# Channel attention and a multiplicative FFN on one core: an order chosen from an account of free times, and seven products instead of eight for half the blocks of the last batch

## The chip, the cores and the metric

The kernel runs on one core of one Trainium2 chip. The metric is the device time of the whole program in microseconds (us), the median of several executions. A second figure, the span, comes from one profiled execution and runs from its first to its last instruction. Engines are named as in the profile: PE (TensorE, matmuls), PEld (its weight loads), DVE (VectorE), ACT (ScalarE), POOL (GpSimd) and SP (SyncE, which here only issues DMAs).

## The reference

```python
def _attn_ref(q, k, v, tau):                      # (4, 5824, 256) each, tau = 1
    qn = q / (np.linalg.norm(q, axis=1, keepdims=True) + 1e-06)
    kn = k / (np.linalg.norm(k, axis=1, keepdims=True) + 1e-06)
    s = kn.transpose(0, 2, 1) @ qn / tau          # 256 x 256 per batch
    s = s - s.max(-1, keepdims=True)
    a = np.exp(s)
    a /= a.sum(-1, keepdims=True) + 1e-09
    return (v @ a).astype(np.float32)

def _moe_ref(x, w1, w2, w3, w_out):               # x: 23296 x 256, d_ff = 1024
    a = x @ w1
    b = x @ w2
    h = a * b @ w3
    return (h @ w_out).astype(np.float32)
```

The result is 23296 x 256 in fp32. The FFN takes the output of the attention as `x`, with its four batches laid one after the other.

## The kernel before

Two foldings make the work small. `w3 @ w_out` is made once (`W_sb`, 1024 x 256, by `w_unit`), and for each batch the 256 x 256 attention matrix is folded into `w1` and `w2` (`fold_mm`; the result is `Wf`). What is left per token is `a = v @ Wf[0]`, `b = v @ Wf[1]`, the product `a * b`, and its product with `W_sb`.

A batch is cut into 12 chunks of tokens (`NCH`): eleven of 512 tokens and a last one of 192. `v` is loaded in pieces of two chunks, turned by a transposing DMA on SP's queue (`transpose_piece`), and used as the moving operand. A block is one chunk `c` and one tile `j` of 128 of the 1024 columns of d_ff, so a full chunk has 8 blocks. `emit_ab` makes a block: two matmuls of 512 columns for `a` and two for `b` (two halves of the 256 input channels, L657), each pair into a PSUM bank of its own; ACT copies `a` to SBUF in bf16 (`as`, L663) and DVE multiplies it with `b` (`abh`, L676). Four PSUM banks, `ab0` to `ab3`, are taken in fixed rotation.

When the 8 blocks of a chunk are done, its product with `W_sb` follows. `emit_half` does it plainly: 32 matmuls of 256 columns. `seven_products` does it by Winograd's form of Strassen's scheme: the 512 x 1024 block and the 1024 x 256 matrix are cut in 2 x 2, four sums of blocks of `abh` are made (`operand`, L589 and L592, tiles `S`; in batches 0 to 2 on POOL, in the last one on DVE), and seven products of 8 matmuls of 128 columns each take the place of eight (L570). ACT copies partial results out (L580), DVE adds others to them (L583), and SP stores the chunk. Before, chunks 0 to 3 of batch 0 and chunk 10 of batch 3 are done plainly, the chunks 11 have a form of their own (`emit_out`), and all others use seven products.

While batch b runs, the scores of batch b+1 are summed between its blocks (`score_units`: matmuls `G` L200, squares on ACT L197, sums `acc` on DVE L212), and near the end of batch b come its softmax and the folds. The last batch has no such work beside it.

The order of the whole program is written out by Python and kept as written; each engine runs its instructions in that order and waits where an operand or a buffer isn't ready. Each block is a slot. What comes between blocks is chosen by counting slots (`pend` for output products with a lag of a few slots, `due_sums` for the sums `S`, `by_slot` for scores) and by a clock that adds up matmul costs (`agenda`, `run_due`: loads, transposes, softmax, folds). No count is kept of when ACT, DVE or POOL will be done.

Of the kernel before, what the change touches and what calls it, by code (L numbers as in the profile page):

```python
# [16 lines left out]
LAG = 2  # L17
LAG_END = 5
LAG_FAST = 4
BIG_BUFS = 21  # L20
# [5 lines left out]
def kernel(  # L26
# [82 lines left out]
    pieces = {}  # L109

# [8 lines left out]
    def load_part(nm, n, pi, lo, hi):  # L119
        nc.gpsimd.dma_start(  # L120
            out=pieces[nm, n, pi][:, lo:hi, :], in_=qk_main[nm, n][0][:, pi * PIECE + lo : pi * PIECE + hi, :]
        )
# [10 lines left out]
    def new_vT(n):  # L133
        vTs[n] = (
            vT_pool.tile([P, NT - 1, CT, P], BF16, tag="vT", name=f"vT_{n}"),
            vT_pool.tile([P, CT, P + LEFT], BF16, tag="vTt", name=f"vTt_{n}"),
        )
# [11 lines left out]
    def transpose_half_on_pe(n, pi, h, on_act):  # L149
        if pi == 0 and h == 0:  # L150
            new_vT(n)
        t = pieces["v", n, pi]
        i0 = 4 * h
        pe_transpose(
            vTs[n][0][:, pi * PIECE + i0 : pi * PIECE + i0 + 4, :, :].rearrange("p i c t -> p (i c) t"),
            [t[:, i0 + i, ct * P : (ct + 1) * P] for i in range(4) for ct in range(CT)],
            "out", on_act,
        )

    def transpose_piece(n, pi):  # L160
        if pi == 0:
            new_vT(n)
        vT, vTt = vTs[n]
        t = pieces.pop(("v", n, pi))
        if pi < NP_ - 1:
            nc.sync.dma_start_transpose(vT[:, pi * PIECE : (pi + 1) * PIECE, :, :], t[:, :, :])
        else:
            g = LAST - 1
            nc.sync.dma_start_transpose(vT[:, pi * PIECE : pi * PIECE + g, :, :], t[:, :g, :])

            first = n % 2 == 0
            nc.sync.dma_start_transpose(vTt[:, :, :P] if first else vTt[:, :, LEFT:], t[:, g, :])
            nc.sync.dma_start_transpose(vTt[:, :, P:] if first else vTt[:, :, :LEFT], t[:LEFT, g + 1, :])
# [6 lines left out]
    def score_units(n):  # L180
# [4 lines left out]
        def pair_unit(pr, part):  # L185
# [7 lines left out]
            if part < 2:  # L193
                if part == 0:
                    sqs[0] = work.tile([P, 2, 2, C], F32, tag="sq", name=f"sq_{n}_{pr}", bufs=2)
                src = qt if part == 0 else kt
                nc.scalar.activation(out=sqs[0][:, :, part, :], in_=src[:, o : o + 2, :], func=AF.Square)  # L197
# [10 lines left out]
            elif pr == 0:  # L208
                if part == 2:
                    nc.vector.tensor_add(accs[n], sqs[0][:, 0], sqs[0][:, 1])  # L210
            else:
                nc.vector.tensor_add(accs[n], accs[n], sqs[0][:, part - 2])  # L212

        sqs = [None]
# [62 lines left out]
    def soft_units(n):  # L277
# [142 lines left out]
        def fold_mm(key, c2, tag="ab", on_act=True):  # L420

            w, c1, lo, hi = key
            if c2 == 0:
                turn = (lo // 512 * 4 + w * CT + c1) % 3
                home = bank(tag) if n == 0 or turn == 2 else {"tag": ("out2", "G")[turn], "bufs": 1}
# [6 lines left out]
            if c2 == CT - 1:  # L432
                dst = Wf[n][:, c1, w, lo:hi]
                if on_act:
# [3 lines left out]

        def fold(i, tag="ab"):
            h, rest = divmod(i, 4)  # L440
            w, c1 = divmod(rest, 2)
# [35 lines left out]
        if n == 0:  # L477
            return [k_first, k_row, q_first, scaled_first, first_folds, second_quarter, sum_start, k_early] + [lambda i=i: fold(i, "ab" if i == 7 else "out") for i in range(4, 8)]
# [12 lines left out]
    clock = [0.0]  # L491
    agenda = []

    def run_due(upto=None):
        lim = clock[0] if upto is None else upto
        while agenda and agenda[0][0] <= lim:
            _, _, cost, fn = agenda.pop(0)
            clock[0] += cost
            fn()

# [9 lines left out]
    pend = []  # L510
# [4 lines left out]
    def rhs_of(b, c, ct):  # L515
        vT, vTt = vTs[b]
        if c < NCH - 1:
            return vT[:, 4 * c : 4 * c + 4, ct, :]
        return vTt[:, ct, :]

    last_ab = [None]
    halves = {}
    slot = [0]
    due_sums = []
    following = []
    comb = {}

    def seven(b, c):
        if b == B - 1:
            return c < NCH - 2  # L530
        return (4 if b == 0 else 0) <= c < NCH - 1

    def combine_weights(step):
# [15 lines left out]
        else:  # L549
            nc.vector.tensor_sub(T[:, 3], b21, f[:, 1])  # L550

    def seven_products(b, c, k1, k2):

        T = comb["T"]
# [5 lines left out]
        t1, t2, t3, t4 = ([T[:, i, j, :] for j in range(4)] for i in range(4))  # L560
        st, sums = {}, {}
        tags = {"A": "out0", "B": "out1", "C": "out1" if b < B - 1 else "out2"}
        adder = nc.gpsimd if b < B - 1 else nc.vector

        def product(nm, a, w, first=False):
# [8 lines left out]
            clock[0] += 8 * (P * MM_COL + MM_FIX)  # L574
# [4 lines left out]
        def keep(r, d):  # L579
            nc.scalar.copy(quarter(r, d), st["A"])  # L580

        def join(nm, r, d):
            nc.vector.tensor_add(quarter(r, d), st[nm], quarter(r, d))  # L583

        def operand(i):

            x = sums[i] = work.tile([P, 4, 2 * P], BF16, tag=f"S{i}", name=f"S{i}_{b}_{c}", bufs=1)
            if i == 1:
                adder.tensor_add(x, a21, a22)  # L589
            else:  # L590
                u, w = {2: (sums.get(1), a11), 3: (a11, a21), 4: (a12, sums.get(2))}[i]
                adder.tensor_sub(x, u, w)  # L592

        def p1():
            st["o"] = work.tile([P, 4, D], F32, tag="o_sb", name=f"osb_{b}_{c}", bufs=3)
            product("A", a11, w1, True)
            keep(0, 0)

        def p5():
            product("C", sums[1], t1, True)  # L600

        def p6():
            product("A", sums[2], t2)
            keep(0, 1)

        def p7():
            product("A", sums[3], t3)
            keep(1, 1)

        def p2():  # L610
            product("B", a12, w21, True)

        def p4():
            product("A", a22, t4)
            keep(1, 0)

        def p3():
            product("C", sums[4], w22)

        def store():  # L620
# [3 lines left out]
        def S(i):  # L624
            return lambda: operand(i)

        def J(*x):
            return lambda: join(*x)

        def then(fn):  # L630
            return lambda: following.append(fn)

        if b == B - 1:
            return [S(1)], [
                [S(2), p1], [S(3), p5], [p6], [S(4), p7], [J("C", 1, 1), p2],
                [J("B", 0, 0), p4], [p3, J("C", 0, 1), store],
            ]
        return [S(1), S(2), S(3), S(4)], [
            [p1], [p2, then(J("B", 0, 0))], [p6], [p5], [p7], [then(J("C", 1, 1))], [p4], [p3, then(J("C", 0, 1)), then(store)],
        ]  # L640

    def gate():

        if last_ab[0] is not None:
            nc.gpsimd.tensor_copy(gate_t, last_ab[0][:1, :1])  # L645

# [4 lines left out]
    def emit_ab(b, c, j):  # L651
        n = chunk_cols(c)
        tiles = []
        for w in range(2):
            t = psum.tile([P, 512], F32, name=f"{'ab'[w]}_{b}_{c}_{j}", **bank("ab"))
# [5 lines left out]
            tiles.append(t)  # L661
        a_sb = work.tile([P, 512], BF16, tag="a_sb", name=f"as_{b}_{c}_{j}", bufs=4)
        nc.scalar.copy(a_sb[:, :n], tiles[0][:, :n])  # L663
        if c == NCH - 1:
            if b % 2 == 0 and j == 0:
                lefts[b // 2] = work.tile([P, FT, 2, P + LEFT], BF16, tag="left", name=f"left_{b}", bufs=1)
            both = lefts[b // 2][:, j, b % 2, :]
            nc.vector.tensor_mul(both, a_sb[:, :n], tiles[1][:, :n])
            ab = both[:, :P] if b % 2 == 0 else both[:, LEFT:]
        else:  # L670
            if j == 0:
                halves[c] = [
                    in_pool.tile([P, 4, 512], BF16, tag="big", name=f"abh_{b}_{c}_{h}", bufs=BIG_BUFS) for h in range(2)
                ]
            ab = halves[c][j // 4][:, j % 4, :]
            nc.vector.tensor_mul(ab, a_sb, tiles[1])  # L676
        last_ab[0] = ab
        slot[0] += 1
        if not seven(b, c):
            if b == B - 1 or c == NCH - 1:  # L680
                lag = LAG if b == B - 1 else FT + LAG_FAST
                pend.append((slot[0] + lag, 1, lambda only=None: emit_out(b, c, j, ab, only)))
            elif j == FT - 1:
                for i in range(FT):
                    fn = lambda i=i, ab2=tuple(halves[c]): emit_half(b, c, i, ab2)
                    pend.append((slot[0] + 1 + LAG_FAST + i, 1, fn))
        elif j == FT - 1:
            sums, groups = seven_products(b, c, *halves[c])
            for i, fn in enumerate(sums):
                due_sums.append((slot[0] + 2 * i, fn))  # L690
            ready = slot[0] + 1 + (LAG_FAST if b < B - 1 else 0)
            for i, group in enumerate(groups):
                wait = 0 if b == B - 1 else i
                pend.append((ready + wait, 2, lambda group=group: [fn() for fn in group]))
        clock[0] += 4 * (n * MM_COL + MM_FIX)

    def emit_half(b, c, i, ab2):
# [13 lines left out]
        clock[0] += 4 * (D * MM_COL + MM_FIX)  # L711
        if i == 3:
            nc.scalar.copy(o[:, 0:2, :], t)
        elif i == FT - 1:
            nc.vector.tensor_copy(o[:, 2:4, :], t)
# [3 lines left out]
    def emit_out(b, c, j, ab, only=None):  # L719
# [23 lines left out]
        clock[0] += len(lhs) * (D * MM_COL + MM_FIX)  # L743
        if j == FT - 1:
            o = work.tile([P, 4, D], F32, tag="o_sb", name=f"osb_{b}_{c}", bufs=3)
# [283 lines left out]
```

## Time and profile before

| | us |
|---|---|
| median of 3 runs (555.11 to 555.23) | 555.18 |
| span of the profiled execution | 553.5 |
| PE busy | 542.1 |
| DVE busy | 435.5 |
| ACT busy | 375.8 |
| POOL busy | 304.8 |
| L657, matmuls of `a` and `b` with 512 columns (x1408) | 418.8 |
| L570, matmuls of the seven products, 128 columns (x2184) | 166.6 |

The median is 1.7 us above the span: this much lies around the instructions. Busy time of PE is not work done: matmuls overlap in the pipeline, a matmul of 512 columns is recorded with 379 ns and one of 128 columns with 219 ns, while the next one starts earlier than that. What a matmul costs on PE is the distance from its start to the start of the next, and that is read from a timeline.

Four batches follow each other: the blocks of batch 0 begin near 37 us, those of batch 1 near 165, of batch 2 near 300 and of batch 3 near 428, and the last matmul starts at 549.2 us. What comes before 37 us is the first batch's loads, scores and softmax.

### The profile page before, as it was taken

To read this page: it belongs to the slowest core of one execution; us is meant where nothing else is said; L and a number is where in the kernel's file an instruction comes from. 1 tells how busy PE (TensorE), PEld (TensorE's weight loads), DVE (VectorE), ACT (ScalarE), POOL (GpSimd) and SP (SyncE) were. 2 spreads that over 40 slices of the span, in tenths; PEclk is the share of its full clock that TensorE was granted. 3 is DMA by queue.
4 is the path that set the end of the run, shared out by engine and by line. 5 is a ranking of instruction groups with operands and counts; after the bars stand their busy time and mean duration, and the time that the engine had idled before them with its cause. 6 is when DMAs were issued, how large, how long until landed. Compare 5 with 4: busy or idle time off the path is not lost.

```text
span 553.5 us, 12330 instructions
## 1 busy us (share of the span) xinstructions
PE 542.1 (98%) x4630; PEld 352.9 (64%) x4630; DVE 435.5 (79%) x789; ACT 375.8 (68%) x757; POOL 304.8 (55%) x257
## 2 busy tenths in 40 slices
PE   7799999999999999999999999999999999999997
PEld 4564577766666666666667566666666666666665
DVE  5567747899976787988876788888877688988984
ACT  5436647788866777777766777777766666566663
POOL 4150022678889678889887588898987400010000
PEclk9999999999999999999999999999999999999999
DMA  9999888975666879576554777875650245343102
GB/s 213 211 206 209 167 164 201 224 180 82 152 140 155 191 150 165 126 147 136 128 127 122 153 153 156 164 147 124 147 115 40 83 117 117 91 110 82 77 40 97
DMA packets 74972, 77.61 MB, mean 140 GB/s; under 512 B 54176, under 2 KB 58784, under 8 KB 74912
## 3 DMA queue, kind: packets, MB, share of 16 engines
q0 software_dynamic: 15616, 38.93, 40.3%
q1 hardware_dynamic: 58928, 37.17, 24.2%
q8 instruction: 36, 0.59, 0.4%
q10 hardware_dynamic: 368, 0.72, 0.3%
q14 instruction: 24, 0.20, 0.1%
HBM read 78.91 MB, written 23.86 MB: 186 GB/s over the span
## 4 chain that ended last, share of the span: by engine, by line
PE 93%; DMA 5%; DVE 0%; ACT 0%; POOL 0%; issue 0%; POOLq 0%
PE a L657 28%; PE b L657 28%; PE prodA L570 13%; PE prodC L570 6%; PE G L200 5%; PE prodB L570 3%; DMA k<-in_k_dram 3%; PE o L707 3%; PE fold L428 2%; DMA q<-in_q_dram 2%; PE o_out L738 2%; PE w L882 1%; PE G L271 0%; PE narrow L452 0%; PE sqq L259 0%
## 5 line engine op out<-in xcount | busy, mean ns | idle before, releaser
L676 DVE TENSOR_TENSOR abh<-as,b 128x512 bf16<-128x512 bf16 x352 | 240.0, 684 | 82.0 <-ACT as L663 76.2
L663 ACT CAST as<-a 128x512 bf16<-128x512 f32 (+1 forms) x384 | 215.4, 562 | 94.8 <-PE a L657 61.5
L657 PE MATMUL a<-vT,Wf 128*128 128x512 bf16 x704 | 209.4, 379 | 0.1
L657 PE MATMUL b<-vT,Wf 128*128 128x512 bf16 x704 | 209.4, 379 | 0.0
L657 PEld LDWEIGHTS <-Wf 128*128 128x128 bf16 x1536 | 141.1, 98 | 100.6 <-issue 0.8
L570 PEld LDWEIGHTS <-S 128*128 128x128 bf16 x1248 | 82.6, 98 | 34.3
L212 DVE TENSOR_TENSOR acc<-acc,sq 128x512 f32<-128x512 f32 x132 | 91.6, 694 | 3.0 <-ACT sq L197 1.9
L580 ACT COPY osb<-prodA 128x256 f32<-128x256 f32 x156 | 58.1, 372 | 42.0 <-PE prodA L570 41.4
L589 POOL TENSOR_TENSOR S<-abh,abh 128x1024 bf16<-128x1024 bf16 x29 | 61.7, 2127 | 32.1 <-DVE abh L676 16.6
L570 PEld LDWEIGHTS <-abh 128*128 128x128 bf16 x936 | 62.0, 98 | 25.7 <-issue 0.2
L592 POOL TENSOR_TENSOR S<-S,abh 128x1024 bf16<-128x1024 bf16 x29 | 61.8, 2131 | 1.9
L592 POOL TENSOR_TENSOR S<-abh 128x1024 bf16<-128x1024 bf16 x29 | 61.8, 2131 | 0.1
L592 POOL TENSOR_TENSOR S<-abh,S 128x1024 bf16<-128x1024 bf16 x29 | 61.7, 2129 | 0.1
L645 POOL COPY gate_t<-abh 1x1 bf16<-1x1 bf16 x39 | 7.2, 185 | 80.1 <-DVE abh L676 79.9
L570 PE MATMUL prodA<-comb_T,S 128*128 128x128 bf16 x624 | 47.6, 219 | 0.0
L200 PE MATMUL G<-k,q 128*128 128x256 bf16 x276 | 47.0, 273 | 0.0
L197 ACT ACTIVATE sq<-q 128x512 f32<-128x512 bf16 x69 | 43.8, 634 | 0.0
L197 ACT ACTIVATE sq<-k 128x512 f32<-128x512 bf16 x69 | 43.4, 628 | 0.0
L583 DVE TENSOR_TENSOR osb<-prodC,osb 128x256 f32<-128x256 f32 x78 | 32.5, 417 | 0.0
L200 PEld LDWEIGHTS <-q 128*128 128x128 bf16 x276 | 23.9, 98 | 3.6
L570 PE MATMUL prodB<-W_sb,abh 128*128 128x128 bf16 x312 | 23.8, 219 | 0.1
L570 PE MATMUL prodC<-comb_T,S 128*128 128x128 bf16 x312 | 23.8, 219 | 0.0
(139 smaller groups left out, 444.0 us busy)
## 6 DMA issues: line engine op xcount, KB each, us to landing
out_dram<-osb SPq DMA_DIRECT2D x44, 512.0 KB, 3.2
k<-in_k_dram POOLq DMA_DIRECT2D x19, 512.0 KB, 8.3
v<-in_v_dram POOLq DMA_DIRECT2D x19, 512.0 KB, 5.2
q<-in_q_dram POOLq DMA_DIRECT2D x18, 512.0 KB, 5.8
w_wout<-in_moe_w_dram POOLq DMA_DIRECT2D x1, 2048.0 KB, 21.6
k<-in_k_dram POOLq DMA_DIRECT2D x4, 320.0 KB, 6.5
v<-in_v_dram POOLq DMA_DIRECT2D x4, 320.0 KB, 5.4
q<-in_q_dram POOLq DMA_DIRECT2D x3, 320.0 KB, 5.2
```

The lines of the kernel that those rows point to most:

```text
L197: nc.scalar.activation(out=sqs[0][:, :, part, :], in_=src[:, o : o + 2, :], func=AF.Square)
L200: nc.tensor.matmul(G[:, ct, :], lhsT=qt[:, i, ct * P : (ct + 1) * P], rhs=kt[:, i, :], start=(pr == 0 and part == 0 and ct == 0), stop=(pr ...
L212: nc.vector.tensor_add(accs[n], accs[n], sqs[0][:, part - 2])
L570: nc.tensor.matmul(st[nm][:, i, :], lhsT=a[:, j, i * P : (i + 1) * P], rhs=w[j], start=(first and j == 0 and i == 0), stop=(j == 3), skip_ ...
L580: nc.scalar.copy(quarter(r, d), st["A"])
L583: nc.vector.tensor_add(quarter(r, d), st[nm], quarter(r, d))
L589: adder.tensor_add(x, a21, a22)
L592: adder.tensor_sub(x, u, w)
L657: nc.tensor.matmul(t[:, :n], lhsT=Wf[b][:, ct, w, j * P : (j + 1) * P], rhs=rhs_of(b, c, ct), start=(ct == 0), stop=(ct == CT - 1),)
L663: nc.scalar.copy(a_sb[:, :n], tiles[0][:, :n])
L676: nc.vector.tensor_mul(ab, a_sb, tiles[1])
L707: nc.tensor.matmul(t[:, k, :], lhsT=ab2[j // 4][:, j % 4, (2 * h + k) * P : (2 * h + k + 1) * P], rhs=W_sb[:, j, :], start=(j == 0 and k = ...
```

## The change

The change does three things.

First, the order. Slots, lags and the clock are replaced by an account of free times: `now` holds a time for PE, ACT, DVE and POOL, `free` one for each PSUM bank, and `work_on` adds the cost of each instruction as it is written. The program is split into lines that stop after each group of matmuls and say when the next group can start: `normal` (a block, in two halves), `by_seven` (below), `seven_products` or `plain_products` (a chunk's output). `step` takes the line that can start first. Banks are taken by `open_bank`, the one that is free first, instead of in rotation; in the last batch `out2` and `G` join the four. Sums on POOL wait in a list (`pool_line`) and are written when POOL is free by the account.

Second, in the last batch chunks 0 to 9 are taken two at a time, and for 4 of the 8 tiles `j` of such a pair `a` and `b` of both chunks come from `by_seven`: seven products of 512 columns instead of eight. It needs four sums of blocks of the turned `v` per pair (`token_sum`, on POOL) and four sums of blocks of `Wf`, once (`weight_sums`, on DVE from the PSUM banks of the folds).

Third, smaller things that come with it. The sums `S` are made on POOL in the last batch too. Five chunks of the last batch are done plainly (0, 2, 6, 9, 10) instead of one. `seven_products` starts its bank B with a copy of A by ACT, which saves one addition on DVE. The turned `v`, the sums `S`, and `w3` with `w_out` move into the common pool of buffers `big` (31 instead of 21), so `w3` and `w_out` are loaded by five DMAs instead of two. Some loads and scores get earlier places.

```diff
+HALF_BACK = 12
-BIG_BUFS = 21
+BIG_BUFS = 31
...
+    BY_SEVEN = {(3, c): 4 for c in range(0, 10, 2)}
+    PLAIN = {0: (0, 1, 2, 3), 1: (), 2: (), 3: (0, 2, 6, 9, 10)}
+    now = {"PE": 0.0, "ACT": 0.0, "DVE": 0.0, "POOL": 0.0}
+    LATE = {"PE": 0.205, "ACT": 0.155, "DVE": 0.135, "POOL": 0.1}
...
+    def work_on(engine, cost, *after):
+        now[engine] = max(now[engine], *after, 0.0) + cost
+        return now[engine] + LATE[engine]
...
+    def token_sum(b, c, i):
...
+        b11, b12, b21, b22 = (rhs_of(b, c + d, ct) for ct in range(CT) for d in range(2))
+        if i == 0:
+            nc.gpsimd.tensor_sub(t[:, 0], b12, b11)
+        elif i == 1:
+            nc.gpsimd.tensor_sub(t[:, 1], t[:, 0], b22)
+        elif i == 2:
+            nc.gpsimd.tensor_sub(t[:, 2], b22, b12)
+        else:
+            nc.gpsimd.tensor_add(t[:, 3], b21, t[:, 1])
...
+    def by_seven(b, c, j):
...
+        xt, X = take(f"X_{b}_{c}_{j}", True)
+        r = mm512(X, W[:, 0, 0, js], rhs_of(b, c, 0), True)
+        yt, Y = take(f"Y_{b}_{c}_{j}", True, True)
+        nc.scalar.copy(Y, X)
...
+        tt, t = take(f"T_{b}_{c}_{j}")
+        r = mm512(t, S[0][:, js], T[:, 0], True)
+        t5 = work.tile([P, 512], F32, tag="t5", name=f"t5_{b}_{c}_{j}", bufs=2)
+        nc.scalar.copy(t5, t)
...
+        r = mm512(X, S[1][:, js], T[:, 1], False)
+        zt, Z = take(f"Z_{b}_{c}_{j}", True, True)
+        nc.vector.tensor_add(Z, X, t5)
...
+        r = mm512(Y, W[:, 1, 0, js], rhs_of(b, c, 1), False)
+        a0 = cast(Y, f"as_{b}_{c}_{j}")
...
+        r = mm512(X, S[2][:, js], T[:, 2], False)
+        b1 = work.tile([P, 512], BF16, tag="b_sb", name=f"bs_{b}_{c + 1}_{j}", bufs=2)
+        nc.vector.tensor_add(b1, X, t5)
...
+        r = mm512(Z, S[3][:, js], rhs_of(b, c + 1, 1), False)
+        h1 = place(b, c + 1, j)
+        nc.vector.tensor_mul(h1, b1, Z)
...
+        r = mm512(X, W[:, 1, 1, js], T[:, 3], False)
+        h0 = place(b, c, j)
+        nc.vector.tensor_mul(h0, a0, X)
...
+    def step(b, todo, sevens, at_n):
...
+        choices = [(max(now["PE"], w.est()), i, w) for i, w in enumerate(lines["W"])]
+        if lines["N"] is not None:
+            choices.append((max(now["PE"], lines["N"].est()) + 0.08, 3, lines["N"]))
+        if outs:
+            hurry = credit[0] > 0.0 or steps_left[0] > 2 * HALF_BACK or not todo
+            choices.append((max(now["PE"], outs[0].est()) + (-0.02 if hurry else 0.2), 4, outs[0]))
...
+        when, kind, line = min(choices, key=lambda x: x[:2])
...
-    SLOTS0, SLOTS = (37, 78), (4, 71)
+    SLOTS0, SLOTS = (37, 76), (3, 66)
...
-            moves = [("qk", n, 1, 1), ("v", b, 2, 7), ("qk", n, 2, 19), ("v", b, 3, 25), ("qk", n, 3, 37)]
+            moves = [("qk", n, 1, 1), ("v", b, 2, 5), ("qk", n, 2, 16), ("v", b, 3, 23), ("qk", n, 3, 31)]
```

## Prediction, made before the changed kernel ran

> **What bounds the kernel now.** I read the page's busy table and its chain of waits first, then PE's waits, then busy time by batch, then one stretch of the timeline.
>
> ```profile
> PE 542.1 (98%) x4630; PEld 352.9 (64%) x4630; DVE 435.5 (79%) x789; ACT 375.8 (68%) x757; POOL 304.8 (55%) x257
> PE 93%; DMA 5%; DVE 0%; ACT 0%; POOL 0%; issue 0%; POOLq 0%
> ```
>
> PE is named in 93% of the chain that ended last, DMA (the first loads) in 5%, DVE, ACT and POOL in none. What PE waited for:
>
> ```profile
> PE sqq L259 <- DMA q<-in_q_dram: 4.7, 4, 1.7
> PE warm_I-94_95 L230 <- DVE ones_pp L87: 1.4, 1, 1.4
> PE sqq L259 <- ACT q L804: 0.4, 1, 0.4
> PE sum L405 <- ACT e L385: 0.4, 1, 0.4
> PE sqk L259 <- DMA k<-in_k_dram: 0.2, 1, 0.2
> ```
>
> All of it lies in the first 37 us, where the change does nothing. By batch (columns: stretch, its length, busy us and count of PE, PEld, DVE, ACT, POOL, granted clock, DMA share, GB/s):
>
> ```profile
> 37.00:165.00 128.00, 128.00 (x974) 82.01 (x974) 103.21 (x174) 91.11 (x176) 60.48 (x60) 1.00 0.85 171
> 165.00:300.00 135.00, 134.92 (x1200) 88.11 (x1198) 108.43 (x201) 100.69 (x209) 112.91 (x81) 1.00 0.69 145
> 300.00:428.00 128.00, 128.00 (x1125) 83.42 (x1123) 103.18 (x188) 95.17 (x196) 104.15 (x75) 1.00 0.62 134
> 428.00:549.00 121.00, 120.98 (x1081) 78.50 (x1079) 99.76 (x178) 72.85 (x148) 9.67 (x12) 1.00 0.32 89
> ```
>
> PE is full in every batch, and in the last one POOL is nearly idle. But pipelined matmuls look busy even when they start late, so I took start-to-start distances: 0.216 us for 512 columns, 0.109 for 256, 0.056 for 128 (medians). Against 2.4 columns per ns plus 2.5 ns for each matmul, all starts from 60 to 549 us together lose 1.6 us, mostly at the joins of the batches. So the middle holds almost no waiting that an order could recover; time falls only with columns.
>
> The latencies for a chain come from a stretch near the end:
>
> ```profile
> 538.24 0.59 PE L657 MATMUL b<-vT,Wf 128*128 128x512 bf16 x2
> 538.44 0.58 ACT L663 CAST as<-a 128x512 bf16<-128x512 f32 x1 [0.72 <-DVE abh L676]
> 538.67 0.61 PE L570 MATMUL prodA<-comb_T,abh 128*128 128x128 bf16 x8
> 539.06 0.69 DVE L676 TENSOR_TENSOR abh<-as,b 128x512 bf16<-128x512 bf16 x1 [0.29 <-ACT as L663]
> 539.12 0.59 PE L657 MATMUL a<-vT,Wf 128*128 128x512 bf16 x2
> ```
>
> The pair for `a` gives way to `b` at 538.24, and ACT begins 0.20 later; ACT takes 0.58, DVE starts 0.04 after it and takes 0.69.
>
> **What the Trainium skill says.** "TensorE: Matmul & The Clock Gate", section "Wait — 56ns, not 53.3ns?", gives start-to-start as N / 2.4 GHz plus about 2.5 ns when warm. The trace agrees (0.216, 0.056). The page "SBUF — State Buffer", section "Who interferes with whom", says that a DVE operation with two SBUF inputs contends with a GpSimd one that reads SBUF, and one with a single SBUF input does not. The change brings GpSimd work into the last batch; the DVE operations of its blocks read one operand from PSUM and one from SBUF. L676, of that kind, shows no effect: 684 ns on average (240.0 us for 352), 59.90 us for its 88 with POOL 84% busy (165 to 300 us) and 60.19 with POOL 8% busy (428 to 549 us). So I add nothing for POOL's presence. "VectorE: DVE Perf Modes", section "The TRN2 errata — SBUF-src ops pay a fixed extra latency per instruction", gives (N+151)/0.96 ns for an fp32 addition, 691 ns at 512; the row of `acc` (L212, one PSUM and one fp32 SBUF operand) shows 694.
>
> **PE's work.** By the order of instructions of the two kernels:
>
> - a and b. 20 pairs of blocks (5 pairs of chunks, 4 tiles each) lose one of 8 matmuls of 512 columns: 20 x 0.2158 = 4.32 us less.
> - Output. Four more chunks are done plainly: 32 matmuls of 256 columns (32 x 0.1092 = 3.49) instead of 56 of 128 (56 x 0.0558 = 3.13): 4 x 0.367 = 1.47 us more.
> - All else is the same on PE: scores, folds, `w_unit`.
>
> Net 2.85 us less. The totals agree: 1245259 columns and 4616 matmuls become 1239115 and 4500, so 6144 / 2400 + 116 x 0.0025 = 2.56 + 0.29 = 2.85.
>
> **The other engines in the last batch**, whose PE stretch shrinks to about 118 us:
>
> - DVE: 99.8, less 40 products of L676 (27.4), 40 sums S (27.4) and 30 additions L583 (12.5); plus 80 operations of the new blocks at 0.69 (55.2) and 12 additions L583 (5.0): 92.7 us, 79%. Back to back such operations start 0.60 apart, so there is more room than this says.
> - ACT: 72.9, plus 20 more copies of 512 net (11.7), less 40 output copies at 0.372 (14.9), plus 30 such for the six chunks of sevens (11.2), plus 8 plain copies at 0.586 (4.7): 85.6 us, 73%. The copy `Y` goes from PSUM to PSUM, which the trace doesn't show; 0.56 (the form mean of L663) to 0.63 (an ACT operation that reads SBUF, L197); I take 0.58.
> - POOL: 24 sums at 2.13 and 20 token sums of half that size at half that time (no row; 0.7 to 1.4, I take 1.07): 72.5 us, 61%.
>
> None becomes the bound on average. The 8 weight sums on DVE (no row; 0.69 to 0.75 by L212 and L437) fall at the end of batch 2, where 4 scalings go to ACT: 3 us more on a DVE with 20% free.
>
> **What the new order adds in waits.** I took each place in PE's order as the sum of what stands before it at the prices above, and compared each hand-over with the latencies read. Three are short:
>
> - A block of sevens copies `X` to `Y` and PE then goes on with `X`: end of the first matmul, 0.20, 0.58, about 0.05, so 0.83. For the pair of chunks 2 and 3 (tile 1) only 0.54 us of other matmuls lie between: 0.29 lost; four others lack 0.08. About 0.3 in sum.
> - At the end, the plain output of chunk 10 comes right behind chunk 9's last group and waits for its copy: 0.3. The last outputs of chunk 11 wait for chunk 10's copy: 0.5. Before, this last wait was 0.18. About 0.6 more.
> - Queueing on ACT and DVE: in the densest 10 us of the last batch DVE has 0.96 of its room taken (counted at 0.60 each). Between 0 (PE is given something else) and 1.5 us; I take 0.3.
>
> POOL's sums come earlier than before: the tightest has over 1 us to spare (before, two were 0.15 late at the end of batch 0), so I give back 0.3 at the joins. Loads for batches 1 and 2 come 2 to 11 us earlier, and the scores end 5 slots earlier, so each piece has about 16 us before its first use. Splitting the load of `w3` into quarters adds three issues on POOL (0.9 each) where POOL has nothing else. If the lead were gone, a late piece would cost its lateness once.
>
> Sum: -2.85 + 0.3 + 0.6 + 0.3 - 0.3 = -1.95. Against the profiled span: 553.55 - 1.95 = 551.6; with the 1.63 us outside the span 553.2.
>
> **Rivals.**
>
> 1. The sum holds, and DVE and ACT hide it all: the waits of the new order are nil, and the joins' losses fall too: -2.85 and up to 1 us more, 551.5 to 552.4. For it: the new order gives PE the next thing that can start. Against it: the three short places are there in the order. It counts as faster.
> 2. Tight order. Hand-overs with under 0.25 us to spare go from 44 to about 100. If each of the 20 blocks of sevens loses 0.1 us through queueing, 2 us go: 555.0, no change that can be measured. For it: three held banks per block. Against it: the busy sums above.
> 3. Slower: DVE takes over as the bound of the last batch. Per pair of chunks PE has 8 normal blocks (6.9), 4 of sevens (6.0) and two chunks of output (6.6), 19.5 us; DVE has 24 operations at 0.69 (16.6) and 2.4 additions L583 (1.0), 17.6. The eight new additions per pair (`Z` and `b1`) decide: they fill DVE's room of 1.9 us at 0.24 more each, so from 0.93 us on PE begins to wait, and at 1.03 each pair loses 0.8 us, 4 in all: 557.2. Against it: L212 is of the same kind and takes 0.694.
>
> **Chances.** The forecast 0.71, rival 1 0.07, rival 2 0.16, rival 3 0.06. A difference of 0.2% (1.1 us) is about what can be told from none. Faster by more than that (below 554.07): 0.78; within: 0.16; slower: 0.06. The range 552.0 to 555.0 takes in rival 1 in part and rival 2's middle.
>
> **What would show it.** Right: PE's total falls by 2.85 us with start-to-start distances as before; the new additions take 0.69; gaps of some tenths before `X` in the last batch and before `o_out` at the end; POOL near 60% there. Wrong: PE waiting for DVE `Z` or `b1` again and again, POOL's `tsum` or `S` as a releaser of PE, or new gaps in batches 0 to 2, whose work is unchanged.

## The result, and the profile of the changed kernel

| | before | after |
|---|---|---|
| median, us (5 runs each, same chip) | 555.20 (555.11 to 555.38) | 553.22 (553.11 to 553.42) |
| span of the profiled execution, us | 553.5 | 551.3 |
| start of the last matmul, us | 549.24 | 547.02 |

The ratio of the times is 0.9964, with a 95% interval of 0.9953 to 0.9975: 2.0 us faster, where 553.2 us was predicted.

The page of the changed kernel, busy time and the chain that ended last, answers the first two lines shown of before:

```profile
PE 539.2 (98%) x4503; PEld 350.8 (64%) x4514; DVE 423.7 (77%) x746; ACT 394.5 (72%) x808; POOL 379.0 (69%) x304
PE 93%; DMA 5%; ACT 0%; issue 0%; POOL 0%; DVE 0%; ACTq 0%; POOLq 0%
```

PE still carries the chain. ACT gained 19 us and POOL 74 us of work and neither appears in it. One detail matters for all that follows: 4503 matmuls stand beside 4514 weight loads, though each matmul has its own load (before: 4630 of both). Eleven matmul records are missing from this trace, and the matmul starts show eleven gaps of exactly one matmul of 512 columns (0.216 us). These are not waits and are left out of the sums below. Ten records are missing in the same way in each of two experiments, the one with five tiles and the one with added DVE load.

What PE waited for, in the trace of after (columns as before: us in total, times, longest):

```profile
PE sqq L269 <- DMA q<-in_q_dram: 4.4, 4, 1.6
PE warm_I-94_95 L240 <- DVE ones_pp L86: 1.4, 1, 1.4
PE sqq L269 <- ACT q L1097: 0.5, 1, 0.5
PE sum L415 <- ACT e L395: 0.4, 1, 0.4
PE o_out L1029 <- ACT osb L1061: 0.3, 1, 0.3
PE sqk L269 <- DMA k<-in_k_dram: 0.2, 1, 0.2
```

One line is new: `o_out`, near the end of the program. This list shows only part of what PE loses, because a matmul that starts late behind another one in the pipeline looks busy. The whole loss comes from the distances between matmul starts, less what the columns need (2.4 columns per ns and 2.5 ns for each matmul):

| PE time lost, us | first 37 us | batch 0 | batch 1 | batch 2 | batch 3 | last 7 us |
|---|---|---|---|---|---|---|
| before | 3.69 | 0.55 | 0.47 | 0.33 | 0.19 | 0.18 |
| after | 3.36 | 0.17 | 0.22 | 0.24 | 1.24 | 0.79 |

The columns need 2.85 us less (the sum in the prediction). With the table: -2.85 of work, -0.72 in batches 0 to 2, +1.05 in batch 3, +0.61 at the end, -0.33 in the first loads, together -2.24; the last matmul starts 2.22 us earlier. The -0.33 can't be put down to the change: a spread of that size, 3.2 to 3.6 us, is in the first 37 us of the kernels with the new order, which are alike up to there.

The stretch that holds nearly all of the last batch, in the trace of after (columns: stretch, length, busy us and count of PE, PEld, DVE, ACT, POOL, granted clock, DMA share, GB/s):

```profile
429.00:548.00 119.00, 117.62 (x937) 74.59 (x938) 90.68 (x153) 78.35 (x162) 75.11 (x51) 1.00 0.34 92
```

POOL went from 9.67 us in the last 121 us to 75 us here, and DVE fell from 99.8 to 91. The operations that the change brought, from the groups of instructions of after (busy us, mean ns of one, idle before it; of the token sums, `tsum`, one group of several):

```profile
L953 DVE TENSOR_TENSOR Z<-X,t 128x512 f32<-128x512 f32 x20 | 13.9, 693 | 0.0
L968 DVE TENSOR_TENSOR abh<-bs,Z 128x512 bf16<-128x512 bf16 x20 | 13.8, 688 | 2.1
L963 DVE TENSOR_TENSOR bs<-X,t 128x512 bf16<-128x512 f32 x20 | 13.7, 684 | 0.0
L975 DVE TENSOR_TENSOR abh<-as,X 128x512 bf16<-128x512 bf16 x20 | 13.6, 680 | 0.1
L942 ACT COPY Y<-X 128x512 f32<-128x512 f32 x20 | 11.5, 575 | 8.5 <-PE X L882 8.4
L640 POOL TENSOR_TENSOR tsum<-vT 128x512 bf16<-128x512 bf16 x4 | 4.6, 1154 | 0.0
```

The four DVE operations of a block take 680 to 693 ns, with POOL busy 63% of the stretch (75.11 of 119). This agrees with what the Trainium skill's page "SBUF — State Buffer", section "Who interferes with whom", says of DVE operations with at most one SBUF input: they don't contend with GpSimd.

The place that the prediction named as 0.29 us short, the block of chunks 2 and 3 with tile 1, in the timeline of after (start, length, engine, line, operation, and in brackets the idle time before it):

```profile
445.50 0.68 DVE L963 TENSOR_TENSOR bs<-X,t 128x512 bf16<-128x512 f32 x1
...
445.67 0.38 PE L882 MATMUL X<-vT,Wf 128*128 128x512 bf16 x1
445.89 0.38 PE L882 MATMUL T<-tsum,wsum 128*128 128x512 bf16 x1
446.14 0.57 ACT L942 COPY Y<-X 128x512 f32<-128x512 f32 x1 [0.66 <-PE X L882]
446.24 0.38 PE L882 MATMUL X<-tsum,Wf 128*128 128x512 bf16 x1
...
446.46 0.27 PE L1029 MATMUL o_out<-W_sb,left 128*128 128x256 bf16 x1
...
446.77 0.39 PE L882 MATMUL X<-tsum,wsum 128*128 128x512 bf16 x1
```

PE fills `X` of this block at 445.67, ACT copies it to `Y` from 446.14 to 446.71, and only then may PE add to `X` again, at 446.77. The matmul before, of 256 columns, needs 0.11 from 446.46 on, so 0.20 us are lost. No idle time is printed for the late matmul, since the recorded end of the one before (446.73) reaches almost to its start. A second loss stands just above: from 445.89 to 446.24 are 0.35 where 0.216 would do. This `X` belongs to the block before; its last product may start when DVE has read the bank for `bs`, which ran from 445.50 to 446.18.

The 1.24 us of batch 3 divide so, each wait put to the operation that ended some 0.05 us before PE went on, and each place named by the start of the matmul before it: 0.20 for this one copy `Y`; 0.34 in three places (445.89, 460.16, 479.46) for `bs` on DVE; 0.27 in two (441.26, 443.49) for a bank that an ACT copy gave back; the remaining 0.43 in pieces under 0.09.

### The profile page after: what moved, and what is told of

Read it like the earlier page. It is cut to its first block, busy times and chain, and to the rows that moved or that the text cites. A ratio compares the mean times of both kernels' runs of the same rounds, so it can differ in the third digit from the quotient of the medians.

```text
span 551.3 us, 12007 instructions
## 1 busy us (share of the span) xinstructions
PE 539.2 (98%) x4503; PEld 350.8 (64%) x4514; DVE 423.7 (77%) x746; ACT 394.5 (72%) x808; POOL 379.0 (69%) x304
## 4 chain that ended last, share of the span: by engine, by line
PE 93%; DMA 5%; ACT 0%; issue 0%; POOL 0%; DVE 0%; ACTq 0%; POOLq 0%
PE a L897 26%; PE b L897 25%; PE prodA L751 11%; PE prodC L751 6%; PE G L208 5%; PE o L991 5%; PE X L882 3%; PE prodB L751 3%; DMA k<-in_k_dram 3%; PE fold L444 2%; DMA q<-in_q_dram 2%; PE o_out L1029 2%; PE w L1176 1%; PE Z L882 1%; PE Y L882 1%; PE T L882 1%
## 5 line engine op out<-in xcount | busy, mean ns | idle before, releaser
L919 DVE TENSOR_TENSOR abh<-as,b 128x512 bf16<-128x512 bf16 x312 | 212.9, 684 | 71.9 <-ACT as L887 52.7
L887 ACT CAST as<-a 128x512 bf16<-128x512 f32 (+1 forms) x344 | 193.0, 562 | 68.7 <-PE a L897 56.6
L897 PE MATMUL a<-vT,Wf 128*128 128x512 bf16 x624 | 185.6, 379 | 0.4
L897 PE MATMUL b<-vT,Wf 128*128 128x512 bf16 x624 | 185.6, 379 | 0.0
L897 PEld LDWEIGHTS <-Wf 128*128 128x128 bf16 x1376 | 124.7, 98 | 80.7 <-issue 0.6
L736 POOL TENSOR_TENSOR S<-abh,abh 128x1024 bf16<-128x1024 bf16 x35 | 74.6, 2130 | 52.0 <-DVE abh L919 42.6
L739 POOL TENSOR_TENSOR S<-abh,S 128x1024 bf16<-128x1024 bf16 x35 | 74.6, 2130 | 0.1
L751 PEld LDWEIGHTS <-abh 128*128 128x128 bf16 x840 | 55.6, 98 | 18.3 <-issue 0.2
L761 ACT COPY osb<-prodA 128x256 f32<-128x256 f32 x105 | 39.0, 372 | 18.3 <-PE prodA L751 18.0
L991 PE MATMUL o<-W_sb,abh 128*128 128x256 bf16 x256 | 36.3, 273 | 0.0
L991 PEld LDWEIGHTS <-abh 128*128 128x128 bf16 x256 | 25.0, 98 | 10.0 <-issue 0.2
```

The lines of the kernel that those rows point to most:

```text
L736: nc.gpsimd.tensor_add(x, a21, a22)
L739: nc.gpsimd.tensor_sub(x, u, w)
L751: nc.tensor.matmul(st[nm][:, i, :], lhsT=a[:, j, i * P : (i + 1) * P], rhs=w[j], start=(first and j == 0 and i == 0), stop=(j == 3), skip_ ...
L761: nc.scalar.copy(quarter(r, d), st[nm])
L887: nc.scalar.copy(a_sb[:, :n], t[:, :n])
L897: nc.tensor.matmul(t[:, :n], lhsT=Wf[b][:, ct, w, j * P : (j + 1) * P], rhs=rhs_of(b, c, ct), start=(ct == 0), stop=(ct == CT - 1),)
```

## The experiments

Each kernel ran beside the kernel before on one chip, but not all on the same chip. The median of before lay between 555.02 and 555.20 throughout, so times of different runs are set side by side. Three questions were open. Is the gain from the new products for `a` and `b`, or from the order and the rest of the change? What ends the gain: DVE, POOL, or the lack of banks? Can the end of the program be mended?

**The rest of the change without the new products.** No block of `a` and `b` by seven products, and the plain chunks of before. The order and the smaller things stay (sums on POOL, the new form of `seven_products`, earlier loads):

```diff
-    BY_SEVEN = {(3, c): 4 for c in range(0, 10, 2)}
+    BY_SEVEN = {}
-    PLAIN = {0: (0, 1, 2, 3), 1: (), 2: (), 3: (0, 2, 6, 9, 10)}
+    PLAIN = {0: (0, 1, 2, 3), 1: (), 2: (), 3: (10,)}
```

> The new order with no blocks of sevens (all a and b by eight products), and the outputs of the last batch by seven products as before (chunk 10 plain). PE has exactly the columns and matmuls of the kernel before. If the gain is columns alone: the joins give back some 0.9 us, the end takes 0.6, so 554.7 to 555.3. If the order brings the gain by itself: 553 to 554. If the order costs and the sevens pay for it: over 555.5.

Measured: 554.78 us (554.47 to 557.03, 13 runs), ratio 1.0 with 0.9992 to 1.0008. PE's columns are those of before. Batches 0 to 2 lose 0.17, 0.22 and 0.23, the same as after, so the 0.72 gained there doesn't come from the new products. Nor does most of the loss at the end, which is 0.63 instead of 0.18. Batch 3 loses 0.04 instead of 0.19. Together some 0.4 us are gained, too little for the times to tell. No run parts the order from the smaller things. The seven products bring the rest: 554.78 - 553.22 = 1.56 for the 20 blocks and the plain chunks that go with them, and the intervals of the two ratios don't overlap. In PE's time this is 2.85 less work against 1.20 more lost in batch 3 and 0.16 at the end.

**The end on other banks.** The outputs of chunk 10 go to `ab0` and `ab1`, the last ones of chunk 11 to `G` and `out2`, instead of `out0` and `out1`, whose copies PE waits for:

```diff
-                for tag in ((("out0", "out2") if b == B - 1 else ("out0", "out1"))[: len(lhs)] if small else ("out0", "out1"))
+                for tag in ((("G", "out2") if b == B - 1 else ("out0", "out1"))[: len(lhs)] if small else (("ab0", "ab1") if b == B - 1 else ("out0", "out1")))
```

> As the changed kernel, but at the end the outputs of chunk 10 go to banks ab0 and ab1 and those of chunk 11 to G and out2, which are free by then, so that neither waits for the copy of the chunk ahead. If these waits (0.29 and 0.51 us in the profile) are on the path: 552.3 to 552.7. If something else holds the end, the copies and stores behind it: 553.1 to 553.3.

Measured: 553.52 us (6 runs), ratio 0.9971 (0.996 to 0.9983), no better than after. The waits of PE in its trace:

```profile
PE o_ab L1029 <- DVE left L915: 1.0, 1, 1.0
```

The wait for ACT's copy is gone, and a longer one has taken its place: `ab0` and `ab1` were held by the last block of all until DVE had multiplied it. The end loses 1.11 instead of 0.79. A bank that is free most of the time isn't free at this moment, so the fixed choice was the fault.

**The end on the banks that the account has free first.**

```diff
...
+            tags = ("out0", "out1")
+            if b == B - 1 and not small:
+                tags = sorted(loose(), key=lambda t: free.get(t, 0.0))[:2]
...
```

> As the changed kernel, but chunk 10's outputs go to the two banks that the account says are free first, and chunk 11's to out0 and out1. The run with fixed banks ab0 and ab1 only exchanged 0.8 us of waits for 1.0 us on a product of chunk 11. If the two waits at the end are on the path: 0.6 to 0.8 less than the changed kernel, 552.4 to 552.7. If the stores behind hold the end: 553.1 to 553.3.

Measured: 552.55 us (552.21 to 553.34, 5 runs), ratio to before 0.9956 (0.9942 to 0.9969), span 550.8. PE's waits in its trace, whole:

```profile
PE sqq L269 <- DMA q<-in_q_dram: 4.7, 4, 1.6
PE warm_I-94_95 L240 <- DVE ones_pp L86: 1.4, 1, 1.4
PE sqq L269 <- ACT q L1099: 0.5, 1, 0.5
PE sum L415 <- ACT e L395: 0.4, 1, 0.4
PE sqk L269 <- DMA k<-in_k_dram: 0.2, 1, 0.2
```

No output waits any more, and the starts of the last 7 us lose nothing (0.79 in after). The last matmul starts 0.59 us earlier than in after, with 0.23 more lost in the first loads. The intervals of the two ratios overlap, so it is the trace that shows this gain, not the times. It is the fastest version that ran, by the medians.

**Six of eight tiles by seven products**, to see whether the gain goes on:

```diff
-    BY_SEVEN = {(3, c): 4 for c in range(0, 10, 2)}
+    BY_SEVEN = {(3, c): 6 for c in range(0, 10, 2)}
```

> As the changed kernel, with 6 instead of 4 of 8 tiles by sevens: PE has 2.16 us less work, VectorE about 13 us more by durations (112 of 114 us). If columns alone count: 551.1. If VectorE becomes the limit of the last batch, as in the slower rival of the prediction: PE waits for Z and b1, 553 to 557.

Measured: 561.35 us, ratio 1.0113 (1.0099 to 1.0127). This is above both expectations. PE has 2.16 us less to do than in after and loses 11.48 us in batch 3 instead of 1.24. Its largest waits for the blocks of batch 3:

```profile
PE X L882 <- DVE Z L953: 1.3, 3, 0.5
PE X L882 <- ACT Y L942: 0.9, 2, 0.6
...
PE T L882 <- ACT as L887: 0.5, 2, 0.2
PE a L897 <- ACT t L948: 0.4, 2, 0.2
```

And the middle of the batch, by windows:

```profile
420.00:510.00 90.00, 85.11 (x636) 49.31 (x635) 77.72 (x134) 62.05 (x130) 63.08 (x46) 1.00 0.37 86
```

DVE is busy 86% of it (77.72 of 90), against 82% in after, and the waits name DVE and ACT in turn: an `X` is given back late because its copy or its addition came late.

**Two of eight**, the same edit with `: 2`.

> As the changed kernel, with 2 instead of 4 of 8 tiles by sevens: PE has 2.16 us more work, VectorE 14 us less by durations. If each block of sevens is worth its saved matmul less about 0.06 us of waits (1.2 us for 20 in the profile): 554.6 to 555.0. If the waits of the last batch come from elsewhere in the order: 555.4.

Measured: 555.01 us (13 runs), ratio 1.0 (0.9992 to 1.0008). PE has 2.16 us more to do than in after and loses 0.79 in batch 3. Half the blocks bring no gain that the times can tell: of the 2.16 us that the ten blocks save, the four added plain chunks take 1.47, and batch 3 loses 0.75 more than without any block (0.04, there without the added plain chunks).

**Five of eight**, on top of the version with the mended end, the same edit with `: 5`.

> The run with free banks at the end, with 5 instead of 4 of 8 tiles by sevens: PE 1.08 us less, VectorE 7 us more (106 of 115 us). If the waits of the last batch grow in proportion to the blocks (1.2 us for 20): 551.7 to 552.0. If 4 of 8 is where VectorE's room ends: 553 to 556.

Measured: 554.11 us (21 runs), ratio 0.9983 (0.9977 to 0.999). PE's work is 1.08 us less than with four, its loss in batch 3 is 4.02 instead of 1.23: 1.6 us slower by the medians, though still a little faster than before. The fifth tile costs 2.79 us of waits and brings 1.08. The window of this run:

```profile
420.00:510.00 90.00, 88.92 (x723) 54.82 (x723) 76.55 (x133) 64.99 (x139) 65.77 (x48) 1.00 0.38 92
```

**DVE loaded by itself.** The changed kernel, with an operation on a buffer that nobody reads behind each of the 20 blocks, and told to the account (so that the order and the banks of the last batch change with it):

```diff
         finish(b, c, j, free[xt])
+        extra = work.tile([P, 768], F32, tag="extra", name=f"extra_{b}_{c}_{j}", bufs=2)
+        nc.vector.memset(extra, 1.0)
+        work_on("DVE", 0.6)
```

> As the changed kernel, with one more DVE instruction after each of the 20 blocks of sevens: a memset of 768 fp32 columns into a buffer that nobody reads, about 0.65 us each, 13 us in all, told to the account as 0.6. VectorE then has the load of the run with six of eight, with the changed kernel's matmuls and banks. If VectorE's throughput is what cost that run its 11 us in the last batch: 8 to 12 us more than the changed kernel, 561 to 565. If banks held and chains of hand-overs of more blocks of sevens did: 0.5 to 3 us more, 553.7 to 556.

Measured: 557.94 us, ratio 1.0051 (1.0038 to 1.0064). The added group and the middle of the batch, in its trace:

```profile
L981 DVE MEMSET extra<- 128x768 f32 x20 | 14.0, 698 | 2.2
```

```profile
420.00:510.00 90.00, 88.14 (x680) 52.59 (x680) 81.45 (x140) 62.42 (x130) 64.79 (x47) 1.00 0.36 86
```

14.0 us more of DVE cost PE 4.72 us (5.96 lost in batch 3). So more load on DVE, with the order that the account makes of it, lets PE wait before DVE is full: it is a cause. It isn't the whole cause of the loss with six tiles: there DVE is less busy (77.72 against 81.45 of the same 90 us) and PE loses nearly twice as much. The measurement fell between the two expectations. What makes the rest, about 5.5 us, goes with the number of blocks; each of them holds three banks through a chain of copies and additions, which is the likely reason, but no run here separates it.

**All outputs by seven products**, to see what the plain chunks are for:

```diff
-    PLAIN = {0: (0, 1, 2, 3), 1: (), 2: (), 3: (0, 2, 6, 9, 10)}
+    PLAIN = {0: (0, 1, 2, 3), 1: (), 2: (), 3: (10,)}
```

> As the changed kernel, with only chunk 10 done plainly in the last batch: PE has 1.47 us less work, GpSimd 34 us more (106 of 115 us). If PE's columns alone count: 551.8. If GpSimd is the reason for the plain chunks: PE waits for S, and the time is 553 to 557.

Measured: 568.31 us, ratio 1.0237 (1.0223 to 1.0251). This is far above both expectations. PE has 1.47 us less to do and loses 19.08 us in batch 3 and at the end together, instead of 2.03. Its waits for POOL, then POOL's timeline before the longest of them, and three lines of PE's behind it:

```profile
PE prodC L751 <- POOL S L739: 7.6, 2, 7.3
...
PE prodA L751 <- POOL S L739: 0.7, 1, 0.7
```

```profile
538.32 2.12 POOL L736 TENSOR_TENSOR S<-abh,abh 128x1024 bf16<-128x1024 bf16 x1
540.52 2.12 POOL L739 TENSOR_TENSOR S<-S,abh 128x1024 bf16<-128x1024 bf16 x1
542.59 2.12 POOL L739 TENSOR_TENSOR S<-abh 128x1024 bf16<-128x1024 bf16 x1
544.66 4.20 POOL L739 TENSOR_TENSOR S<-abh,S 128x1024 bf16<-128x1024 bf16 x2
```

```profile
548.92 1.04 PE L751 MATMUL prodC<-W_sb,S 128*128 128x128 bf16 x8 [7.29 <-POOL S L739]
...
553.91 1.06 PE L751 MATMUL prodA<-comb_T,S 128*128 128x128 bf16 x8
555.43 0.61 PE L751 MATMUL prodA<-comb_T,abh 128*128 128x128 bf16 x8 [0.46 <-ACT osb L761]
```

POOL runs without a pause and ends at 548.86; PE goes on at 548.92, after 7.3 us of waiting. One reason is in the order on POOL: the last sum of chunk 8 was written behind all four of chunk 9, and each engine takes its instructions in the order written. The plain chunks therefore are relief for POOL: each gives up 0.37 us of PE to spare POOL four sums, 8.5 us (4 x 2.13).

Not all of the loss is waiting for POOL. The waits that name POOL come to 8.3 us (7.6 + 0.7). Behind the long one, matmuls of 128 columns start 0.107 us apart until 554.66, where elsewhere it is 0.056: eight of them take 1.06 us and not 0.61. The granted clock of the stretch from 548.9 to 555 us is 0.50. These slow starts cost some 2.1 us (42 x 0.051). The rest, smaller gaps from the start of the batch on, isn't put to an engine here.

**One plain chunk less**, on the version with the mended end: `3: (0, 2, 9, 10)`.

> The same with chunk 6 also done by seven products: PE 0.37 us less, GpSimd 8.5 us more (80 of 116 us). If GpSimd has room there: 0.2 to 0.4 less than the run with free banks. If its sums already come late: as long or longer.

Measured: 553.06 us, ratio 0.9963 (0.9951 to 0.9976). PE's work falls by 0.37 us and its loss in batch 3 rises from 1.23 to 2.16, so the last matmul starts 0.58 us later; the intervals of the two ratios overlap. One line is new among its waits:

```profile
PE prodA L751 <- POOL S L739: 0.3, 1, 0.3
```

This product starts 0.45 late, at 521.02. Most of the other new loss stands in the 5 us just before it, at matmuls of `b` and of a block by seven products, and isn't traced to POOL. So four additional sums on POOL already reach PE, by a little.

**The account without latencies.** The instructions stay the same; only the estimate of when a result reaches the next engine is set to nothing, and so the order and the choice of banks change:

```diff
-    LATE = {"PE": 0.205, "ACT": 0.155, "DVE": 0.135, "POOL": 0.1}
+    LATE = {"PE": 0.0, "ACT": 0.0, "DVE": 0.0, "POOL": 0.0}
```

> As the changed kernel, with the four latencies between engines (0.205, 0.155, 0.135 and 0.1 us) set to 0 in the account, so that the order is chosen as if a result could be used at once. The work is the same on every engine. If the account's accuracy is what keeps the sevens from waiting: PE waits for copies and additions in the last batch, 556 to 562. If any sensible interleaving would do: 553.0 to 554.2.

Measured: 565.57 us (565.34 to 565.71), ratio 1.0189 (1.0175 to 1.0202): 12.3 us slower than after and more than expected, with the same work on every engine. PE loses 12.33 us in batch 3, and 0.79 and 1.01 in batches 1 and 2. Of its waits:

```profile
PE X L882 <- DVE bs L963: 1.0, 4, 0.4
PE X L882 <- DVE Z L953: 0.7, 3, 0.3
```

An order by account of free times is worth no more than the latencies in it. Without the new products, the account and the smaller things bring some 0.4 us; with them, the latencies in the account decide between -2 and +10 us.

The number of tiles per pair, side by side (DVE's busy share is that of the stretch 420 to 510 us; the last matmul's start tells what is left of the gain). The row of five has the mended end, worth 0.6:

| tiles by seven | PE's work against four | PE loses in batch 3 | DVE busy | last matmul, us |
|---|---|---|---|---|
| 2 | +2.16 | 0.79 | 71% (64.23) | 548.70 |
| 4 | 0 | 1.24 | 82% (74.13) | 547.02 |
| 5 | -1.08 | 4.02 | 85% (76.55) | 547.99 |
| 6 | -2.16 | 11.48 | 86% (77.72) | 555.32 |
| 4 and added DVE load | 0 | 5.96 | 91% (81.45) | 551.78 |

## Why the prediction was right, point by point

**The bound and PE's work.** Right: PE was the bound before and is after, and the last matmul moved by what PE's columns and losses add up to. The -2.85 stands, with the same start-to-start distances. The totals behind it are a little low: the trace of before holds 4630 matmuls and 1249414 columns where the prediction has 4616 and 1245259. The difference between the kernels, 116 matmuls and 6144 columns, is the same where no records are missing, as in the run with the mended end.

**The joins.** Predicted -0.3, measured -0.72 (0.55 + 0.47 + 0.33 before, 0.17 + 0.22 + 0.24 after). The step looked only at the POOL sums that had been late and gave back their part; the change took away other small losses in those batches too, and the run without the new products shows that it does so without them.

**Waits in the last batch.** Predicted 0.6 in two terms of 0.3 (short hand-overs and queueing), measured 1.05. The hand-over counted as 0.29 short lost 0.20, and no other copy `Y` stands among the larger gaps, so that term (0.3) was good. The mis-sized term is the queueing on ACT and DVE, where 0.3 was taken from a range of 0 to 1.5: the three waits for `bs`, the two for ACT's banks and the small pieces are 0.34 + 0.27 + 0.43 = 1.04, less the 0.19 that batch 3 lost before, 0.85. This error, +0.55, met that of the joins, -0.42; the time came out as close as it did partly because the two cancelled. That is luck, and so are the 0.33 less lost in the first loads, which nothing in the prediction accounts for.

**The end.** Predicted 0.6, measured 0.61. The two places are the named ones: 0.29 us at 541.20, where chunk 10 waits for chunk 9's copy, and 0.51 at 544.87, where the last outputs wait for chunk 10's. Giving these outputs the banks that are free first removes both; giving them other fixed banks does not.

**The other engines.** DVE was put at 92.7 us for the last batch; the stretch of 119 us shows 90.68. POOL was put at 72.5 with token sums of 1.07; they take 1.15, and the stretch shows 75.11. ACT was put at 85.6 and came to 78.35. The count of copies was right: a chunk by seven products has five of 256 columns on ACT (for 35 chunks the trace has 140 of L761 and 35 of L774). What differs is the measure. The prediction added durations, while busy time counts a stretch once where an operation starts before the recorded end of the one ahead. The durations of the same stretch add up to 85.2. None of it reached PE. The copy `Y` from PSUM to PSUM took 575 ns where 0.58 was taken, the additions 684 and 693 where 0.69 was. The 0.56 given there for L663 is a mean over two widths; its copies of 512 columns take 584 ns.

**Rival 1**, all hidden: false as such, 1.05 us of waits are there. The end is the part of it that can be had (552.55).

**Rival 2**, 0.1 per block by queueing: half of it. 1.05 over 20 blocks is 0.05 each, and it didn't take the gain.

**Rival 3**, DVE takes over: its price is refuted, 0.69 and not 1.03. Its mechanism is real and close: with 14 us more of DVE work PE loses 4.7 us more. With one tile in eight more it loses 2.8 more, and there DVE's part isn't separated from that of the banks held. Its threshold was drawn wrongly, though. It had PE wait only once DVE's work exceeded PE's; in the runs with five and six tiles and with the added load DVE was busy for 85 to 91%.

**A step that was too generous.** "None becomes the bound on average" was true and proved less than it seemed: for POOL it was 63% of the last batch, and one chunk's sums more already reached PE.

## What to carry to other kernels

When one engine is full and the others are at 70 to 80%, price a trade of its work for theirs as the saved columns minus the late hand-overs, each taken from a timeline, and look for the step at which the waits grow faster than the saving: here between four and five tiles of eight, well before any helper was full. Choose order and buffers from an account that contains the measured hand-over latencies; without these, the same instructions in another order ran 12 us longer. For the last outputs of a program, take the buffer that is free first at that moment rather than one by name.

## What was not expected of the hardware

- The token sums on POOL, 128x512 in bf16, take 1.154 us, more than half of the 2.13 us for 128x1024. An estimate from these two sizes: some 0.18 us (2 x 1.154 - 2.13) of each operation don't depend on its length.
- A copy by ACT of 512 fp32 columns from PSUM to PSUM (575 ns) costs slightly less than the same from PSUM to SBUF (593 ns, L948), and matmuls then add to the copied bank: `Y` in 20 blocks, and `prodB` of the outputs, whose 256-column copy takes 359 ns against 372 for L761 to SBUF.
- After PE had waited 7.3 us in the run with all outputs by seven products, matmuls of 128 columns started 0.107 us apart instead of 0.056 for 5.7 us, at a granted clock of 0.50. In no other run did PE pause for more than 1.2 us after the first 37 us, and none of them shows this, so how long a pause it takes stays open.
